# A list of 1250 steps for one core, in another order and with other engines for some of its copies

## The chip, the core and the metric

The kernel runs on one core of a Trainium2 chip. Five engines of that core work side by side, each on its own queue and in the order of that queue: TensorE (PE, matmuls and transposes; PEld in the profile is its weight load), VectorE (DVE), ScalarE (ACT), GpSimd (POOL) and SyncE (SP, here only a queue of DMA issues). The metric is the time of one execution on the device in microseconds; a kernel's time is the median of its runs.

## The reference

Eight batches of eight heads, 576 positions, 64 values per head. Attention is causal, with a bias from the running sum of a per-position gate; its output, as 8 x 576 rows of 512, goes through a layer norm and a two-layer MLP with a residual.

```python
scores = scale * q @ k.T                                  # 8 batches x 8 heads, 576 x 576
cum = cumsum(maximum(s, 0))                               # along the positions
scores = where(causal, -1e9, scores + minimum(-(cum[:, None] - cum[None, :]), 0))
attn = softmax(scores)
x = (attn @ v)  as 8 x 576 x 512                          # heads side by side
xn = (x - mean(x)) / sqrt(var(x) + 1e-6) * g_ln
out = x + maximum(xn @ w_ch1, 0) @ w_ch2                  # 512 -> 2048 -> 512
```

## The kernel before

**The work.** Positions are cut into four tiles of 128 and a tail of 64; the tails of two batches share one tile (`xm`). Batch 0 and 1 put the bias into four extra rows of the key and query matrices. Batches 2 to 7 work with the bias in the values: v is multiplied by a weight per key position (`weigh_v`, L233), two columns behind it hold the weight itself in two parts (`weigh_ones`, L245 and L246), and the sums of these columns divide the result. From batch 2 on, two heads go together as a "burst".

**One burst** `B2.n` (n = 4 x batch + pair): six PSUM banks of scores, transposed, by matmuls (`sa`, `sb`, `sc`, L553); six exponentials on ACT into `er` (`bx`, L560); four causal masks on POOL (`bm`, L497); then for each head P·V into a bank `pot` (`Y`, L626), and its normalization on DVE (`K`: `sums` L643, `rinvs` L644, `xb` L645). The 64-position tails of all heads of a batch have their own steps: copies of the tail keys into a zeroed matrix on POOL (`tk`, L145), matmuls `sd` (L524), an exponential (`se`), a mask (`sm`), P·V (`Z`) and normalization (`z`).

**Loads.** From batch 3 on, f32 rows of q and k come by SP (`lr`, L206, tile `rowtmp`), are cast on POOL (`cr`, L218), and are transposed by DMA (`tr`, L225). v rows come by SP (`lv`, L206, with six buffers) and go through `weigh_v` (`vm`). Earlier batches load by POOL's own DMA queue, and PE transposes them, with copies out of PSUM on ACT or DVE (L141 on ACT, L143 on DVE; words `E`, `G`, `y`, and `O2` for a copy in SBUF ahead of it).

**Norm and MLP.** `ga` are the statistics (L700), `la` one tile's normalization `xn` (L741), `Da` the transposing DMA. An MLP chunk is a queue of 32 units: 16 of "h" (L792, bank `ph`, with a relu into `hT`, L783 on ACT or L781 on DVE) and four times four quarters of "y" (L811, bank `py`, evicted by `yo`, L823, on DVE, and stored by SP). The words `u` and `U` take the next unit of the queue; the letter sets the engine of the relu, and does nothing for a "y" unit. For the first chunk some units are done by tile, as `M` (matmuls) and `r` (relu).

**What sets the order.** Nothing is scheduled: the kernel walks a string of words, `PLAN`, and each word issues its instructions at once to the queues of their engines. A word `name.args:E` names a step of the table `STEPS`; the letter behind the colon is the engine of a copy, a cast or a weighing (A, D, P). So an engine's order is the order of the words. PSUM banks are taken from pools as they come free: until the word `to` there are banks m (2), s (3), t (2), o (1); behind it m (2) for `py`, `pot` and the tails' `pott`, and s (6) for scores, `sd` and `ph`. A word that takes a bank waits on its engine until the bank's last reader is done.

Ahead of the walk, the kernel before issues a prologue of loads and memsets in plain code.

```python
for word in PLAN.split():
    step, _, eng = word.partition(":")
    name, *args = step.split(".")
    args = [int(c) if c.isdigit() else c for c in args]
    STEPS[name](*args, *([E[eng]] if eng else []))
```

## Time and profile before

| | us |
|---|---|
| median of three runs | 345.44 (345.36, 345.44, 347.5) |
| the profiled execution | 344.55 |
| its span on the core | 343.1 |
| around the span | 1.45 |

| engine | busy us | share | instructions |
|---|---|---|---|
| PE | 330.4 | 96% | 3093 |
| DVE | 202.3 | 59% | 568 |
| ACT | 186.5 | 54% | 347 |
| POOL | 167.4 | 49% | 305 |

Times are in microseconds unless marked ns. The profile is of one execution. A row of a group reads: line, engine, operation, what it writes and reads, shapes, count, then the busy time and the mean ns of one, then the engine's idle time just before these instructions and what ended it. A row of a wait reads: who waited, for whom, the sum, how many times, the longest. A row of the chain or the timeline begins with the start and the duration. In a row by stretches, the stretch and its length come first, then each engine's busy time with the number of its instructions, then PE's clock (1.00 is full speed), the share of the DMA engines and GB/s. The granted clock is 0.997 over the span.

### The profile page before, as it was taken

The page shows a single profiled execution, that of the slowest core. Times are in us where ns is not written, and L with a number is a line of the kernel's source. Part 1 is how long each engine was busy: PE and PEld are TensorE (multiplying, and loading weights), DVE is VectorE, ACT ScalarE, POOL GpSimd, SP SyncE. Part 2 cuts the span into 40 slices and gives each one's busy share as a digit, 9 for nine tenths or more (in the row PEclk, how much of TensorE's full clock was granted, in tenths as well). Part 3 has the DMA queues.
Part 4 walks back from the last instruction along what each step waited for, and adds up shares of the span by engine and source line. Part 5 has one row for each costly group of instructions (what it writes and reads, how often), then busy time and mean ns, then how long its engine had stood idle before and what let it go on. Part 6 is the DMA issues. An engine that isn't in the chain of part 4 may idle for free.

```text
span 343.1 us, 8037 instructions
## 1 busy us (share of the span) xinstructions
PE 330.4 (96%) x3093; PEld 183.0 (53%) x3117; DVE 202.3 (59%) x568; ACT 186.5 (54%) x347; POOL 167.4 (49%) x305
## 2 busy tenths in 40 slices
PE   6999999999989999999999999999999999999994
PEld 2899765545544555545555545554455444444443
DVE  6688787957685577357543664566348624533512
ACT  4888899668746676457736774486344204202200
POOL 8897578777379862884774377441301001000000
PEclk9999999999999999999999999999999999999998
DMA  9999999899999999999988976700510141011022
GB/s 142 178 192 182 201 195 208 192 192 253 182 218 213 213 207 201 201 231 214 214 178 201 215 108 151 139 2 2 121 65 2 24 129 46 3 71 51 3 61 66
DMA packets 147962, 48.59 MB, mean 142 GB/s; under 512 B 135280, under 2 KB 143760, under 8 KB 147920
## 3 DMA queue, kind: packets, MB, share of 16 engines
q1 hardware_dynamic: 121856, 38.34, 54.3%
q0 software_dynamic: 24304, 8.92, 22.2%
q10 hardware_dynamic: 1760, 0.79, 1.0%
q8 instruction: 25, 0.41, 0.5%
q14 instruction: 17, 0.14, 0.1%
HBM read 37.11 MB, written 9.44 MB: 136 GB/s over the span
## 4 chain that ended last, share of the span: by engine, by line
PE 72%; POOL 9%; DMA 8%; DVE 4%; SPq 3%; issue 2%; ACT 1%; POOLq 0%; ACTq 0%
PE ph L792 30%; PE py L811 28%; DMA v_bf<-in_v_dram 5%; PE pot L626 4%; SPq L206 3%; PE sa L553 2%; POOL v_bf L233 2%; POOL v_bf L192 1%; DVE xn L741 1%; DMA rowtmp<-in_q_dram 1%; DMA rowtmp<-in_v_dram 1%; ACT er L560 1%; PE sb L553 1%; PE sc L553 1%; PE pott L664 1%
## 5 line engine op out<-in xcount | busy, mean ns | idle before, releaser
L811 PE MATMUL py<-w_bf,hT 128*128 128x512 bf16 (+2 forms) x584 | 128.9, 367 | 2.7 <-DVE yo L823 1.0
L792 PE MATMUL ph<-xT,w_bf 128*128 128x512 bf16 x480 | 109.8, 379 | 0.0
L783 ACT ACTIVATE hT<-ph 128x512 bf16<-128x512 f32 x102 | 60.9, 605 | 78.8 <-PE ph L792 77.1
L811 PEld LDWEIGHTS <-hT 128*128 128x128 bf16 x608 | 55.9, 98 | 60.9 <-issue 1.1
L792 PEld LDWEIGHTS <-w_bf 128*128 128x128 bf16 x544 | 51.4, 98 | 56.4
L497 POOL TENSOR_SCALAR_AFFINE_SELECT er<-er 128x256 bf16<-128x256 bf16 x96 | 38.1, 412 | 52.3 <-ACT er L560 37.7
L823 DVE SCALAR_TENSOR_TENSOR yo<-py,rstd,xb 128x512 f32<-128x512 f32 x32 | 23.9, 749 | 50.7 <-PE py L811 46.2
L560 ACT ACTIVATE er<-sb 128x512 bf16<-128x512 f32 x48 | 28.1, 607 | 20.9 <-PE sb L553 20.9
L781 DVE TENSOR_SCALAR hT<-ph 128x512 bf16<-128x512 f32 x34 | 23.4, 690 | 27.0 <-PE ph L792 25.1
L560 ACT ACTIVATE er<-sa 128x512 bf16<-128x512 f32 x48 | 28.6, 607 | 14.8 <-PE sa L553 14.6
L233 POOL TENSOR_TENSOR v_bf<-rowtmp,wt 128x512 bf16<-128x512 f32 (+1 forms) x30 | 32.9, 1104 | 4.3 <-DMA rowtmp<-in_v_dram 4.1
L560 ACT ACTIVATE er<-sc 128x512 bf16<-128x512 f32 x48 | 28.7, 611 | 4.1 <-PE sc L553 4.1
L741 DVE SCALAR_TENSOR_TENSOR xn<-xb,mv,gb 128x512 bf16<-128x512 f32 x28 | 25.9, 925 | 1.0
L715 POOL TENSOR_TENSOR rstd<-rstd,mhalf 128x4 f32<-128x4 f32 (+1 forms) x8 | 8.8, 1095 | 34.7 <-DVE rstd L714 33.2
L700 DVE BATCH_NORM_STATS2 stats<-xb 128x6 f32<-128x128 f32 (+1 forms) x84 | 24.6, 326 | 0.6
L626 PEld LDWEIGHTS <-er 128*128 128x128 bf16 x480 | 19.7, 97 | 9.5 <-POOL er L497 0.6
L218 POOL CAST kq<-rowtmp 128x512 bf16<-128x512 f32 (+1 forms) x30 | 18.3, 619 | 13.2 <-DMA rowtmp<-in_k_dram 12.3
L643 DVE TENSOR_REDUCE sums<-pot 128x4 f32<-128x8 f32 x48 | 7.8, 162 | 27.0 <-PE pot L626 26.7
L626 PE MATMUL pot<-v_bf,er 128*128 128x66 bf16 x480 | 22.1, 193 | 0.1
L645 DVE TENSOR_TENSOR xb<-pot,rinvs 128x256 f32<-128x256 f32 x48 | 20.4, 424 | 1.7
L553 PEld LDWEIGHTS <-kq 64*128 64x128 bf16 x384 | 11.9, 94 | 9.6 <-issue 3.8
L1017 ACT ACTIVATE er<-st 128x512 bf16<-128x512 f32 x24 | 13.2, 603 | 1.5 <-PE st L1008 1.5
(178 smaller groups left out, 394.8 us busy)
## 6 DMA issues: line engine op xcount, KB each, us to landing
out_dram<-yo SPq DMA_DIRECT2D x32, 256.0 KB
rowtmp<-in_v_dram SPq DMA_DIRECT2D x24, 256.0 KB
rowtmp<-in_k_dram SPq DMA_DIRECT2D x20, 256.0 KB
rowtmp<-in_q_dram SPq DMA_DIRECT2D x20, 256.0 KB
w_bf<-in_moe_w_ch_dram POOLq DMA_DIRECT2D x8, 512.0 KB, 9.2
kp<-in_k_dram POOLq DMA_DIRECT2D x8, 144.0 KB, 9.0
qp<-in_q_dram POOLq DMA_DIRECT2D x8, 144.0 KB, 9.0
v_bf<-in_v_dram POOLq DMA_DIRECT2D x8, 128.0 KB, 7.8
```

The lines of the kernel that those rows point to most:

```text
L233: e.tensor_tensor(out=v_bf[b % 2][0:pn, t, :, 0:D], in0=loaded.pop(("v", b, t))[0:pn], in1=wt[0:pn, t, b, :].unsqueeze(2).to_broadcast([pn ...
L497: nc.gpsimd.affine_select(out=out, in_=out, compare_op=ALU.is_ge, fill=0.0, base=0, pattern=pattern, channel_multiplier=-1,)
L553: nc.tensor.matmul(a, lhsT=lhsT, rhs=rhs, start=True, stop=True)
L560: nc.scalar.activation(out=er[:, 2 * n % 4 + i, o : o + 512], in_=bank["B", n].pop((name, i)), func=ACT.Exp, scale=scale,)
L626: nc.tensor.matmul(pot[:, t, :], lhsT=e[:, o : o + P], rhs=v_bf[b % 2][:, kb, h, :], start=(kb == 0), stop=(kb == t),)
L700: nc.vector.bn_stats(out=st[b][:, t, part, :], in_=x_tiles(b)[t][:, lo:hi])
L741: nc.vector.scalar_tensor_tensor(out=xn, in0=tiles[t], scalar=mvs[b][:, t, 0:1] if b > 0 else mean0[:, t : t + 1], in1=gb, op0=ALU.subtrac ...
L781: nc.vector.tensor_scalar_max(out=dst, in0=ph, scalar1=0.0)
L783: nc.scalar.activation(out=dst, in_=ph, func=ACT.Relu)
L792: nc.tensor.matmul(ph, lhsT=w1_bf[:, kd, fb * P : (fb + 1) * P], rhs=xT[:, :, kd, :], start=(kd == 0), stop=(kd == KD - 1),)
L811: nc.tensor.matmul(py[t], lhsT=hT[:, fb, t * P : (t + 1) * P], rhs=w2_bf[:, fb, c0:c1], start=(fb == 0), stop=(fb == FB - 1),)
L823: nc.vector.scalar_tensor_tensor(out=yo, in0=py[t], scalar=rs, in1=x[:, c0:c1], op0=ALU.mult, op1=ALU.add)
```

## The change

The prologue's loads and memsets become words of the list. They stand as its first 55 words in the order of the code before, and the 37 words behind them are the first 37 of the old list. Behind these 92 the words are the same ones in another order, and some have another engine's letter: 28 copies, casts and weighings, among them fifteen `vm` and four `vo` (batches 2, 3, 4, 6) from POOL to DVE; and of the relu units forty go from ACT to DVE and twenty-four from DVE to ACT. The matmuls are the same.

`piece` takes its bank with whichever of a tile's four column blocks comes first, since they can now stand in any order.

```diff
-    nc.sync.dma_start(out=c_first, in_=s_rows[:, 0 : 2 * P])
-    ld_tile("q", 0, nc.scalar)
-    ld_tile("k", 0, nc.sync)
...
-    ld_cast_tile("k", 1)
-    ld_cast_tile("q", 1)
-    ld_cast_v(0, 0)
...
+    def fill(i):
+        if i == 0:
+            nc.vector.memset(zeros.bitcast(F32), 0.0)
+        elif i == 1:
+            nc.vector.memset(warm, 0.0)
+            nc.scalar.activation(out=warm[:, 1:2], in_=warm[:, 0:1], func=ACT.Exp)
...
+        elif i == 11:
+            nc.gpsimd.memset(rinvs[:, 0, :, NF], 1.0)
+
+    def first_sums(i):
+        if i == 0:
+            nc.sync.dma_start(out=c_first, in_=s_rows[:, 0 : 2 * P])
+        else:
+            nc.sync.dma_start(out=c_in[:, 2 * P : S], in_=s_rows[:, 2 * P : S])
...
-    E = {"A": "act", "D": "dve", "P": "pool"}
+    E = {"A": "act", "D": "dve", "P": "pool", "S": "sync"}
...
     def piece(c, t, j):
-        if j == 0:
+        if ("M", c, t) not in bank:
             bank["M", c, t] = ptile("m", [P, 4, P], "ph")
...
+        "w1": ld_w1,
+        "f": fill,
+        "c": first_sums,
+        "lc": ld_cast_tile,
+        "LV": ld_cast_v,
...
     PLAN = """
-        relu.0 scan.0 relur.1 O cq hi.0 scan.1 ck.0 sub.0 mid.0 lo.0 m hi.1 tc.0 bc.0 sub.1 W.2 T.0.1 relur.2
...
+        c.0 lt.q.0:A lt.k.0:S c.1 f.0 f.1 W.9 f.2 f.3 f.4 f.5 f.6 I lc.k.1 lc.q.1 LV.0.0 lc.k.2 lc.q.2 mT LV.0.1
...
```

**DVE ahead of burst 8** (the first of batch 2). In both pieces `rinvs`, `xb` and `xm0` are the normalization of a head of batch 1 (L602 to L611), `kq1` is a copy of transposed q or k out of PSUM, `stats` the layer norm's statistics. The kernel before:

```order
L143 COPY kq1_110<-trqk_1159 64x2x288
L602 RECIPROCAL rinvs_114<-pot_1215 128x5
L604 TENSOR_TENSOR xb_914<-pot_1215,rinvs_114 128x4x64
L611 TENSOR_SCALAR xm0_117<-pot_1215,rinvs_114 64x64
L718 BN_AGGR mv_222<-stats_221 128x2
L700 BN_STATS stats_1259<-xb_914 128x6
L602 RECIPROCAL rinvs_114<-pot_1261 128x5
L604 TENSOR_TENSOR xb_914<-pot_1261,rinvs_114 128x4x64
L611 TENSOR_SCALAR xm0_117<-pot_1261,rinvs_114 64x64
```

The changed kernel at the same heads:

```order
L781 TENSOR_SCALAR hT_101<-ph_1194 128x512
L602 RECIPROCAL rinvs_114<-pot_1228 128x5
L604 TENSOR_TENSOR xb_946<-pot_1228,rinvs_114 128x4x64
L611 TENSOR_SCALAR xm0_117<-pot_1228,rinvs_114 64x64
L700 BN_STATS stats_1247<-xb_946 128x6
L143 COPY kq1_110<-trqk_1186 64x2x288
L781 TENSOR_SCALAR hT_101<-ph_1250 128x512
L602 RECIPROCAL rinvs_114<-pot_1262 128x5
L604 TENSOR_TENSOR xb_946<-pot_1262,rinvs_114 128x4x64
L611 TENSOR_SCALAR xm0_117<-pot_1262,rinvs_114 64x64
L700 BN_STATS stats_1247<-xb_946 128x6
L781 TENSOR_SCALAR hT_101<-ph_1296 128x512
```

Three relus, which ACT had, now stand between the normalizations.

**POOL ahead of the tails of batch 3.** `c3_122<-kq1_110` are the two copies of the tail keys for which `sd` waits; L233 are weighings of v of batch 3, L218 casts of q and k rows, L497 masks. The kernel before:

```order
L218 CAST kq2_111<-rowtmp_1520 64x512
L497 AFFINE_SELECT er_116<-er_116 128x2x128 x6
L218 CAST rowb_123<-rowtmp_1695 128x512
L497 AFFINE_SELECT er_116<-er_116 128x2x128 x2
L218 CAST rowb_123<-rowtmp_1586 128x512
L233 TENSOR_TENSOR v_bf1_108<-rowtmp_1866,wt_113 128x8x64
L233 TENSOR_TENSOR v_bf1_108<-rowtmp_1921,wt_113 64x8x64
L233 TENSOR_TENSOR v_bf1_108<-rowtmp_1893,wt_113 128x8x64
L145 COPY c3_122<-kq1_110 64x4x64 x2
```

The changed kernel:

```order
L497 AFFINE_SELECT er_116<-er_116 128x2x128 x3
L218 CAST rowb_123<-rowtmp_1631 128x512
L497 AFFINE_SELECT er_116<-er_116 128x2x128
L218 CAST kq2_111<-rowtmp_1520 64x512
L497 AFFINE_SELECT er_116<-er_116 128x2x128 x3
L145 COPY c3_122<-kq1_110 64x4x64 x2
```

No weighing stands ahead of the copies now.

**DVE in batch 5.** `yo` are evictions of the MLP's second layer, `sums`, `rinvs` and `xb` the normalization of a head of batch 4, `v_bf1_108<-rowtmp` a weighing of v of batch 5. The kernel before:

```order
L823 SCALAR_TENSOR_TENSOR yo_2796<-py_2779,rstd_103,xb_1701 128x512
L823 SCALAR_TENSOR_TENSOR yo_2830<-py_2800,rstd_103,xb_1701 128x512
L643 TENSOR_REDUCE sums_2874<-pot_2833 128x4
L644 RECIPROCAL rinvs_114<-sums_2874 128x4
L645 TENSOR_TENSOR xb_2670<-pot_2833,rinvs_114 128x4x64
L643 TENSOR_REDUCE sums_2894<-pot_2883 128x4
L644 RECIPROCAL rinvs_114<-sums_2894 128x4
L645 TENSOR_TENSOR xb_2670<-pot_2883,rinvs_114 128x4x64
```

The changed kernel:

```order
L823 SCALAR_TENSOR_TENSOR yo_2809<-py_2787,rstd_103,xb_1727 128x512
L233 TENSOR_TENSOR v_bf1_108<-rowtmp_2767,wt_113 128x8x64
L643 TENSOR_REDUCE sums_2865<-pot_2854 128x4
L644 RECIPROCAL rinvs_114<-sums_2865 128x4
L645 TENSOR_TENSOR xb_2666<-pot_2854,rinvs_114 128x4x64
L233 TENSOR_TENSOR v_bf1_108<-rowtmp_2743,wt_113 128x8x64
L643 TENSOR_REDUCE sums_2898<-pot_2882 128x4
L644 RECIPROCAL rinvs_114<-sums_2898 128x4
L645 TENSOR_TENSOR xb_2666<-pot_2882,rinvs_114 128x4x64
```

Two weighings, which stood on POOL, are now in DVE's row, each ahead of a normalization.

More of the change, by code (lines that the diff above doesn't have):

```diff
@@ L1318, in fast_path @@
         "lp": ld_cast_pair,
+        "w1": ld_w1,
+        "f": fill,
+        "c": first_sums,
+        "lt": lambda kind, t, eng: ld_tile(kind, t, nc.scalar if eng == "act" else nc.sync),
+        "lc": ld_cast_tile,
+        "LV": ld_cast_v,
+        "I": lambda: make_identity(nc, ident),
+        "mT": make_mask,
+        "g": lambda: nc.gpsimd.dma_start(out=gb, in_=moe_g_ln.partition_broadcast(P)),
+        "cr2": const_rows,
+        "fv": lambda i: nc.gpsimd.memset(v_bf[i][TL:P, NF, :, :], 0.0),
@@ L1319, in fast_path @@
+        "fk": lambda i: nc.gpsimd.memset(kq[i][0:KA, 0, :, S:SP], 0.0),
     }
     PLAN = """
[L1322 to L1325 removed]
```

242 lines of the change are left out of this document (111 added, 131 removed).

## The prediction

> **What bounds the kernel now.** I read the page first: the share of each engine, the slices, the chain that ended last.
>
> ```profile
> span 343.1 us, 8037 instructions
> PE 330.4 (96%) x3093; PEld 183.0 (53%) x3117; DVE 202.3 (59%) x568; ACT 186.5 (54%) x347; POOL 167.4 (49%) x305
> ...
> DMA  9999999899999999999988976700510141011022
> ...
> PE 72%; POOL 9%; DMA 8%; DVE 4%; SPq 3%; issue 2%; ACT 1%; POOLq 0%; ACTq 0%
> ```
>
> TensorE (PE) is busy 96% of the span and is 72% of the chain; no other engine passes 59%. The row of DMA is full up to slice 18 (154 us), so in the first half of the kernel a load can be late. An average over stages hides where an engine is tight, so the second view is the busy time by stretches (the stretch, its length, then PE, PEld, DVE, ACT, POOL).
>
> ```profile
> 0.00:10.00 10.00, 7.36 (x31) 3.44 (x32) 6.27 (x24) 4.61 (x9) 8.86 (x17) 1.00 1.17 150
> 30.00:40.00 10.00, 9.47 (x174) 8.05 (x172) 8.41 (x21) 8.97 (x17) 5.85 (x10) 1.00 1.72 186
> 40.00:50.00 10.00, 10.00 (x145) 7.18 (x144) 8.31 (x20) 9.53 (x21) 6.22 (x14) 1.00 1.26 197
> 50.00:60.00 10.00, 9.72 (x117) 6.04 (x116) 6.95 (x24) 9.18 (x18) 8.53 (x19) 1.00 1.24 207
> 60.00:70.00 10.00, 9.35 (x79) 4.94 (x78) 9.76 (x17) 5.51 (x9) 7.97 (x14) 1.00 0.74 168
> 180.00:250.00 70.00, 69.58 (x649) 36.14 (x650) 39.57 (x117) 42.87 (x81) 31.44 (x59) 1.00 0.58 116
> 330.00:343.10 13.10, 8.42 (x71) 5.45 (x69) 2.70 (x6) 0.00 (x0) 0.00 (x0) 0.93 0.34 81
> ```
>
> This gives a ceiling for any reordering. PE is idle 343.1 − 330.4 = 12.7 us; 10 − 7.36 = 2.64 of that lies in the first 10 us, whose list is the same in both, and 13.10 − 8.42 = 4.68 in the end, where the last output is stored. Left are 5.4 us (a busy PE is not PE at its peak, so this is not exact, but nothing in the rows lets me count more). The set of PE's matmuls doesn't change. The rows also say where others are tight: DVE and ACT from 30 to 70 us, DVE most of all from 60 to 70. From 180 us on, DVE has 30 of 70 us free.
>
> The third view is the chain in order of time, for the two places at which it leaves PE for long.
>
> ```profile
> 58.70 0.42 DVE xb L604
> 59.48 0.81 DVE stats L700 x3
> 60.46 0.80 DVE xn L741
> 61.26 0.41 DVE stats L700 x2
> 61.96 1.65 DVE xn L741
> 63.60 0.80 issue
> 64.71 0.75 DVE yo L823
> 65.64 0.96 DVE xn L741
> 67.11 1.42 DVE xn L741
> 68.53 0.67 DVE kq L143
> 69.20 1.33 DVE yo L823 x2
> 70.57 0.38 PE py L811
> ...
> 90.71 1.77 SPq L206
> 92.53 4.18 DMA rowtmp<-in_v_dram
> 96.77 2.54 POOL v_bf L233 x2
> 99.31 0.81 POOL c L145
> 100.17 0.41 POOL c L145
> 100.63 0.41 PE sd L524 x8
> 101.03 0.86 PE py L811 x4
> ```
>
> At 58.7 to 70.6 us the end hangs on VectorE's (DVE) row: four normalizations, an eviction, a copy, two evictions, with hardly a gap. At 90.7 to 100.6 us a load of v lands, GpSimd (POOL) weighs v, and only behind that, since its row is in order, copies the tail keys for which the `sd` matmuls wait.
>
> **The change, part by part.** The prices come from the groups of instructions (busy time, mean of one) and the waits:
>
> ```profile
> L783 ACT ACTIVATE hT<-ph 128x512 bf16<-128x512 f32 x102 | 60.9, 605 | 78.8 <-PE ph L792 77.1
> L781 DVE TENSOR_SCALAR hT<-ph 128x512 bf16<-128x512 f32 x34 | 23.4, 690 | 27.0 <-PE ph L792 25.1
> L233 POOL TENSOR_TENSOR v_bf<-rowtmp,wt 128x512 bf16<-128x512 f32 (+1 forms) x30 | 32.9, 1104 | 4.3 <-DMA rowtmp<-in_v_dram 4.1
> L741 DVE SCALAR_TENSOR_TENSOR xn<-xb,mv,gb 128x512 bf16<-128x512 f32 x28 | 25.9, 925 | 1.0
> L643 DVE TENSOR_REDUCE sums<-pot 128x4 f32<-128x8 f32 x48 | 7.8, 162 | 27.0 <-PE pot L626 26.7
> L645 DVE TENSOR_TENSOR xb<-pot,rinvs 128x256 f32<-128x256 f32 x48 | 20.4, 424 | 1.7
> L644 DVE RECIPROCAL rinvs<-sums 128x4 f32<-128x4 f32 x48 | 8.6, 179 | 1.6
> L143 DVE COPY xT<-trx 128x512 bf16<-128x512 bf16 x1 | 0.4, 425 | 0.5 <-PE trx L774 0.5
> ...
> POOL v_bf L233 <- DMA rowtmp<-in_v_dram: 4.1, 2, 2.3
> PE sd L524 <- POOL c L145: 1.2, 1, 1.2
> PE pot L590 <- DMA v_bf<-in_v_dram: 0.5, 2, 0.3
> ```
>
> *Loads and memsets as words.* The first 55 words issue what the prologue issued, in its order, and the 37 behind them are unchanged: 0.
>
> *The stall at 100 us.* The POOL piece above shows it: the copies of the tail keys of batch 3 (`c3_122<-kq1_110`) stood behind three weighings of batch 3 and now stand behind masks and casts; of batch 3's five weighings two now run on DVE, the rest come later. The PE wait of 1.2 us goes: −1.2. Next late there would be the masks behind them, at 0.4 us each, within the 0.86 us of a quarter of `py` beside `sd`. If nothing goes, 0.
>
> *More work on DVE before burst 8.* In the row up to the second eviction `yo`, DVE gets three more relus (3 × 0.69 = 2.07), a relu of the first batch's pieces (of the same shape, 0.69), one more `xT` copy (0.43), the eight small operations of two `weigh_ones` (no DVE row for them; by L643 and L644, 0.16 to 0.18 each, 1.4), and a copy of a pair (no DVE row; between 0.43 for the `xT` copy and 0.69, I take 0.6). That is 5.2 us. From 30 to 70 us DVE is busy 8.41 + 8.31 + 6.95 + 9.76 = 33.4 of 40, so 6.6 are free, of which 6.3 before 60. What comes before 55 us (the relus and the `xT` copy, 3.2) I hide in that idle time; the two `weigh_ones` and the pair copy (2.0) fall into the stretch in which the chain runs on DVE without a gap, and land in full. The bounds are 0 and 5.2. ACT gets three relus fewer (3 × 0.605 = 1.8) in a stretch in which it is 92% busy; the chain gives ACT 1%, so I take no gain.
>
> *Slow normalizations.* They take 0.75 us where nothing runs beside them and up to 2.5 where POOL does, as DVE's and POOL's timeline shows:
>
> ```profile
> 60.46 0.80 DVE L741 SCALAR_TENSOR_TENSOR xn<-xb,mv,gb 128x512 bf16<-128x512 f32 x1
> 61.96 2.52 DVE L741 SCALAR_TENSOR_TENSOR xn<-xb,mv,gb 128x512 bf16<-128x512 f32 x1
> ...
> 61.79 1.04 POOL L233 TENSOR_TENSOR v_bf<-rowtmp,wt 128x512 bf16<-128x512 f32 x1
> 62.77 1.16 POOL L218 CAST kq<-rowtmp 128x512 bf16<-128x512 f32 x2
> ```
>
> The four of 58.7 to 70.6 us are 0.80 + 2.52 + 0.96 + 1.42 = 5.7 against 4 × 0.75 = 3.0. POOL keeps casts and two weighings near there but loses the `weigh_ones`; I take a third of the 2.7 us, −0.8 (0 to −2.7).
>
> *Fifteen weighings on DVE.* No DVE row shows one. The nearest is `xn`, also two operands from SBUF and 512 elements: 0.75 to 0.93 us, against 1.1 on POOL. Fifteen take 11 to 14 us, and DVE has the room: 202.3 of 343.1 us are taken. The Trainium skill (SBUF — State Buffer, "Who interferes with whom") states that a DVE operation with two inputs in SBUF and a GpSimd operation that reads SBUF exclude each other, whichever comes first; the row of 2.52 us agrees, and by this rule each moved weighing would go on blocking POOL, or being blocked, which adds to the sum only where the two rows are short of room: at most one mask of 0.41 us at burst 9. What matters more is that DVE's row is in order. The DVE piece above shows the place: the weighing of `rowtmp_2767` now stands ahead of `sums`, `rinvs`, `xb` of the next head and of the next eviction, and in the list only six quarters of `py` (6 × 0.86 = 5.2 us) and a burst of scores lie between its load and it. A load took 1.77 us to issue and 4.18 to land above, 5.95 together, so there is no slack when SP is late, and POOL waited up to 2.3 us for such a load. Counted in the same way, two of the fifteen stand less than 7 us of PE work behind their load, five 9 to 11, eight further. Behind it PE has two quarters of `py` (2 × 0.86) less the 0.77 us of the normalization (0.162 + 0.179 + 0.424), about 1 us of cover. I take +0.5 here (0 to 2.3 − 1.0 = 1.3).
>
> *POOL at burst 21.* Ahead of the mask for which a P·V step of burst 21 waits, POOL now has four casts and a weighing more closely packed (some 3.7 us in a row by 0.6 a cast, `1.16 x2`, and 1.1 a weighing). I take +0.5 (0 to 1.2, the stall that the same kind of queue made at 100 us). The two weighings left on POOL that follow their loads most closely (of batches 3 and 4) have five relu units or more (some 4 us) between them and the P·V steps that need the masks behind them: 0.
>
> *Later first use of v of batch 1.* It stands further behind in PE's order, two units or so; the waits of L590 (0.5 in all) shrink: −0.3 (0 to −0.5).
>
> The relus that change sides behind that (13 more on DVE, 0.69 against 0.605) wait for PE anyway, 77.1 and 25.1 us in their rows: 0. The loads of k and q and the transposes of later batches keep their distance to the bursts that need them within about a unit, 0.86 us; SP's queue is where a delay would start, and its price is that of the loads above: 0 here, the rest in rival B.
>
> Sum: −1.2 + 2.0 − 0.8 + 0.5 + 0.5 − 0.3 = +0.7. The profiled execution took 344.55 us (the span and 1.45 around it), 0.9 below the median of 345.44, so the forecast is 344.55 + 0.7 + 0.9 = **346.1 us**. With all low ends at once the change is −1.2 + 0 − 2.7 + 0 + 0 − 0.5 = −4.4, with all high ends 0 + 5.2 + 0 + 1.3 + 1.2 + 0 = +7.7. The ends won't meet, so I take half the way to each for the forecast's own range: −1.9 to +4.2, 343.6 to 349.6.
>
> **Rivals.** A change below 1%, 3.45 us, can hardly be told from none here; I call faster below 342.0 and slower above 348.9.
>
> *A: the waits go and nothing replaces them.* The stall (−1.2), the normalizations (−2.7), the v waits (−0.5), and the new DVE work finds its idle time: 345.44 − 4.4 = 341.0. For it: 6.6 us free on DVE against 5.2, and the stall plainly goes. Against it: it needs four fifths of all the PE idle time there is in the middle (5.4), while bank evictions stand in the same DVE row. Chance 0.17.
>
> *B: weighings on DVE wait for their loads.* One mechanism: DVE's row stops at a weighing whose `rowtmp` hasn't landed, the evictions `sums`/`xb` and `yo` behind it don't free PE's two banks, PE stops. It costs up to 1.3 us a time beyond the cover; seven of fifteen stand 11 us or less behind their load, and DMA is full up to 154 us. It decides slower when at least three wait in full: 3 × 1.3 + 0.7 = +4.6, 350.0. For it: POOL already waited 4.1 us for v loads in its own row. Against it: two waits only, and eight of the fifteen stand far behind their load. Chance 0.13.
>
> *C: DVE becomes the bound up to burst 9.* All 5.2 us land: −1.2 + 5.2 − 0.3 + 0.5 = +4.2, 349.6. For it: 9.76 of 10 busy at 60 to 70 us. Against it: the added relus stand at 40 to 55 us, with 1.6 to 3 us free in each ten. Chance 0.08.
>
> *D: nothing that shows.* PE's list hides both gains and costs, within half a microsecond of 345.4. It shares its sign with the forecast's neighbours. Chance 0.22; my forecast has the remaining 0.40.
>
> **Numbers.** The forecast's own range, 343.6 to 349.6, with D and C's lower part holds some 0.65; to reach 0.8, the range takes in A's upper and B's lower half: 341.5 to 350.0. Faster by over 1%: A but for its upper part, 0.14, and 0.02 from the forecast's lower end, 0.16. Slower by over 1%: B 0.12, C 0.05 and 0.03 of the forecast's upper end, 0.20. Within 1%: 0.64.
>
> **What would show it.** The `sd` wait on `c L145` at 100 us is absent from the waits. DVE is over 9 in each ten us from 40 to 70 and the DVE stretch of the chain that ends at 70.6 us ends 0.5 to 1.5 us later. A row "DVE v_bf L233 <- DMA rowtmp" with one or two waits, longest below 2.3; with five or more B is right. `xn` means below 0.9. If PE's idle time between 10 and 330 us falls below 2 us, A is right; if it stays at 5 to 6, the forecast is. I am wrong in kind if the difference lies behind 180 us, where I see nothing that could change it.

## The result: slower by two thirds of a per cent, and where it went

The changed kernel takes 347.05 us (median of 22 runs, 346.27 to 349.0); the kernel before took 345.31 in 22 runs of the same occasion (342.69 to 349.68). The ratio is 1.0064, 95% interval 1.0041 to 1.0086: a real loss of about 2 us, within the 1% that was called no change, and inside the forecast's range (346.1, from 341.5 to 350.0). Ratios, and the ranges of runs given further down, leave disturbed runs out (two runs of the experiments took 572 and 610 us), so that a ratio can differ a little from the quotient of the medians.

The profiled execution took 347.48 us, its span is 2.8 us longer than before: PE's last matmul ends 2.3 us later, and the other 0.5 lies behind it. The page's first lines, the answers to those quoted of before:

```profile
span 345.9 us, 8050 instructions
PE 331.7 (96%) x3091; PEld 182.4 (53%) x3117; DVE 225.6 (65%) x618; ACT 176.7 (51%) x328; POOL 149.7 (43%) x274
```

The work moved as the words say: DVE +23 us, POOL −18, ACT −10; PE is the bound as before. For the rest I read one number at each burst: **PE's lag**, the time at which the burst's first `sa` matmul starts, less the time that all of PE's steps ahead of it in the list take at their undisturbed prices (a burst 0.77 us, a P·V 0.30, the tails 0.42 and 0.75, a quarter or a relu unit 0.86, and so on). The matmuls are the same in all kernels, so a step up between two bursts is PE waiting there, or, in four traces of the experiments, PE at half its clock for 3.4 us, which is said where it comes. In us, worked out from the start of those matmuls in each trace:

| burst | 8 | 9 | 12 | 13 | 14 | 16 | 19 | 20 | 31 |
|---|---|---|---|---|---|---|---|---|---|
| before | 9.8 | 10.2 | 10.7 | 12.0 | 12.1 | 12.1 | 12.5 | 12.7 | 13.6 |
| changed | 9.8 | 10.7 | 11.1 | 11.0 | 12.1 | 12.7 | 13.6 | 14.1 | 15.9 |

The step of 1.3 us before burst 13 is gone, and new ones stand elsewhere: 0.5 more than before at burst 9, 1.1 at 14, 0.5 at 15, 0.5 at 19, 0.6 at 20, 0.6 at 25 and 0.2 at 29. With the gain at burst 13, and less some 0.4 of small steps that the kernel before has at the same bursts, they make the 2.3 us at burst 31. The waits of PE of 0.3 us and more in the changed kernel, from 10 us to 330 us:

```profile
PE pot L626 <- DVE v_bf L233: 0.8, 1, 0.8
PE py L811 <- DVE yo L823: 0.8, 1, 0.8
PE pot L626 <- POOL er L497: 0.6, 2, 0.3
PE ph L792 <- DMA xT<-xn: 0.5, 1, 0.5
PE pot L1043 <- ACT er L1002: 0.4, 2, 0.2
PE pot L626 <- DVE xb L645: 0.3, 1, 0.3
```

The `sd` wait isn't among them; P·V (`pot` L626), which waited for nothing worth a row before, now waits for a weighing on DVE, for masks on POOL, and for a bank that a late normalization holds. The largest, at 104.2 us, in the timelines of PE, DVE and POOL of the changed kernel (start, duration, engine):

```profile
104.18 0.23 PE L626 MATMUL pot<-v_bf,er 128*128 128x66 bf16 x2
105.24 0.40 PE L626 MATMUL pot<-v_bf,er 128*128 128x66 bf16 x8 [0.82 <-DVE v_bf L233]
...
99.69 0.75 DVE L233 TENSOR_TENSOR v_bf<-rowtmp,wt 128x512 bf16<-128x512 f32 x1
103.53 1.66 DVE L233 TENSOR_TENSOR v_bf<-rowtmp,wt 128x512 bf16<-128x512 f32 x1
...
102.03 0.60 POOL L218 CAST rowb<-rowtmp 64x512 bf16<-64x512 f32 x1
102.60 2.03 POOL L233 TENSOR_TENSOR v_bf<-rowtmp,wt 128x512 bf16<-128x512 f32 x2
104.60 1.10 POOL L497 TENSOR_SCALAR_AFFINE_SELECT c<-c 64x512 bf16<-64x512 bf16 x1
```

The fifteen weighings on DVE by themselves (min, median, max; first and last start):

```profile
L233 DVE TENSOR_TENSOR v_bf<-rowtmp,wt x15: 670/683/1660, 71.4 to 237.0; 128x512 bf16<-128x512 f32 x13, 64x512 bf16<-64x512 f32 x2
```

The usual one takes 0.68 us; this one took 1.66 while POOL was at two weighings until 104.6, and the first mask behind them took 1.10 (its kind takes 0.65 elsewhere). Below, **the lock** stands for this: a DVE and a POOL operation on SBUF that keep each other waiting. Not all of the 0.82 us is its work. The list has three of the four weighings that this P·V needs directly ahead of it (`vm.3.3:P vm.3.2:P vm.3.1:D bx.13.2 Y.12.0`), and the second one on POOL ends at 104.6; a weighing of 0.68 us on DVE would have ended at 104.2, so that by these rows some 0.6 us are the lock's and the rest the order's.

### The profile page after: what moved, and what is told of

It is laid out like the page before. It is cut to its first block, busy times and chain, and to the rows that moved or that the text cites. A ratio compares the mean times of both kernels' runs of the same rounds, so it can differ in the third digit from the quotient of the medians.

```text
span 345.9 us, 8050 instructions
## 1 busy us (share of the span) xinstructions
PE 331.7 (96%) x3091; PEld 182.4 (53%) x3117; DVE 225.6 (65%) x618; ACT 176.7 (51%) x328; POOL 149.7 (43%) x274
## 5 line engine op out<-in xcount | busy, mean ns | idle before, releaser
L783 ACT ACTIVATE hT<-ph 128x512 bf16<-128x512 f32 x86 | 51.5, 599 | 95.6 <-PE ph L792 93.8
L497 POOL TENSOR_SCALAR_AFFINE_SELECT er<-er 128x256 bf16<-128x256 bf16 x96 | 40.6, 440 | 38.2 <-ACT er L560 31.7
L781 DVE TENSOR_SCALAR hT<-ph 128x512 bf16<-128x512 f32 x50 | 34.0, 688 | 29.2 <-PE ph L792 27.4
L560 ACT ACTIVATE er<-sc 128x512 bf16<-128x512 f32 x48 | 28.2, 614 | 10.1 <-PE sc L553 5.3
L218 POOL CAST kq<-rowtmp 128x512 bf16<-128x512 f32 (+1 forms) x30 | 19.6, 665 | 23.2 <-DMA rowtmp<-in_q_dram 14.4
L741 DVE SCALAR_TENSOR_TENSOR xn<-xb,mv,gb 128x512 bf16<-128x512 f32 x28 | 24.5, 873 | 1.0
L626 PEld LDWEIGHTS <-er 128*128 128x128 bf16 x480 | 19.2, 97 | 10.3 <-issue 1.7
L626 PE MATMUL pot<-v_bf,er 128*128 128x66 bf16 x480 | 22.4, 193 | 2.0 <-DVE v_bf L233 0.8
L233 POOL TENSOR_TENSOR v_bf<-rowtmp,wt 128x512 bf16<-128x512 f32 (+1 forms) x15 | 15.9, 1061 | 5.3 <-ACT hT L783 5.2
L553 PEld LDWEIGHTS <-kq 64*128 64x128 bf16 x384 | 11.9, 94 | 11.0 <-issue 5.8
L218 POOL CAST rowb<-rowtmp 128x512 bf16<-128x512 f32 (+1 forms) x20 | 12.3, 630 | 4.5 <-DMA rowtmp<-in_k_dram 4.4
```

Of the source, the lines that this page charges most:

```text
L218: nc.gpsimd.tensor_copy(out=rows[b % 2][0:pn, t, u], in_=loaded.pop(("kq"[u], b, t))[0:pn])
L497: nc.gpsimd.affine_select(out=out, in_=out, compare_op=ALU.is_ge, fill=0.0, base=0, pattern=pattern, channel_multiplier=-1,)
L560: nc.scalar.activation(out=er[:, 2 * n % 4 + i, o : o + 512], in_=bank["B", n].pop((name, i)), func=ACT.Exp, scale=scale,)
L626: nc.tensor.matmul(pot[:, t, :], lhsT=e[:, o : o + P], rhs=v_bf[b % 2][:, kb, h, :], start=(kb == 0), stop=(kb == t),)
L741: nc.vector.scalar_tensor_tensor(out=xn, in0=tiles[t], scalar=mvs[b][:, t, 0:1] if b > 0 else mean0[:, t : t + 1], in1=gb, op0=ALU.subtrac ...
L781: nc.vector.tensor_scalar_max(out=dst, in0=ph, scalar1=0.0)
```

## The experiments

All of them change words of the list or one instruction; the line numbers are those of the kernel that was edited. Lags at the same bursts, one trace each. With the words of the kernel before up to burst 8, kernels reach it with lags of 8.0 to 9.9, so a difference of 2 us there says little, and the steps say more:

| | 8 | 9 | 12 | 13 | 14 | 16 | 19 | 20 | 31 |
|---|---|---|---|---|---|---|---|---|---|
| before | 9.8 | 10.2 | 10.7 | 12.0 | 12.1 | 12.1 | 12.5 | 12.7 | 13.6 |
| before, a second trace | 8.9 | 8.9 | 9.5 | 11.1 | 11.2 | 11.3 | 12.1 | 14.8 | 15.7 |
| tails first | 9.7 | 9.7 | 10.3 | 10.2 | 12.5 | 12.5 | 12.9 | 13.4 | 14.3 |
| tails first, xn later | 8.6 | 8.6 | 9.1 | 9.1 | 9.2 | 9.9 | 10.5 | 14.8 | 15.7 |
| the same, second trace | 8.7 | 8.8 | 10.1 | 10.0 | 10.6 | 10.9 | 11.3 | 15.6 | 16.5 |
| three parts | 8.0 | 8.0 | 8.6 | 8.5 | 8.6 | 9.2 | 9.7 | 9.6 | 10.5 |
| the same, second trace | 9.9 | 9.9 | 10.5 | 10.4 | 10.5 | 11.8 | 13.3 | 14.0 | 14.9 |
| before with weighings on DVE | 9.7 | 9.7 | 11.6 | 11.9 | 12.0 | 12.0 | 12.4 | 12.3 | 13.2 |
| before, one operand in `xn` | 9.8 | 9.9 | 10.4 | 11.6 | 11.7 | 11.7 | 12.1 | 12.6 | 13.5 |
| changed | 9.8 | 10.7 | 11.1 | 11.0 | 12.1 | 12.7 | 13.6 | 14.1 | 15.9 |
| changed, six places mended | 9.5 | 10.2 | 10.5 | 10.4 | 11.0 | 11.8 | 13.8 | 13.7 | 15.1 |
| changed, weighings back | 10.1 | 11.5 | 15.8 | 15.7 | 17.8 | 17.9 | 19.7 | 20.6 | 23.0 |
| changed, early relus back | 11.8 | 12.5 | 12.8 | 12.8 | 13.9 | 14.5 | 15.2 | 15.4 | 16.8 |
| changed, all engines as before | 12.5 | 13.2 | 17.4 | 17.3 | 21.1 | 21.2 | 22.6 | 23.4 | 28.4 |

### Order and engines apart

First, the changed kernel's order with weighings and `weigh_ones` back on POOL:

```diff
- vm.2.2:D vm.2.1:D vm.3.0:D vm.3.1:D vm.4.3:D vm.4.4:D vm.5.1:D vm.5.3:D vm.5.0:D vm.5.2:D
- vm.6.3:D vm.6.1:D vm.6.4:D vm.7.0:D vm.7.3:D vo.2:D vo.3:D vo.4:D vo.6:D
+ (the same words, in the same places, with :P)
```

> The changed kernel with its fifteen weighings and four weigh_ones back on POOL, and nothing else undone: its order and its relus stay. Theory (weighings and weigh_ones in DVE's row cost PE about 1.9 us, at 70.4, 110.8 and 142.0 us; but the order lists those of batch 3 so late that POOL needs them in a row): those three gaps go, the gap at 104.2 us grows from 1.0 to about 2 us, and the kernel takes 346.1 (345.5 to 346.7). Rival 1 (the order is at fault and the engine isn't): 347.0 or more, the gaps stay with POOL as the one waited for. Rival 2 (all of the loss comes from DVE's weighings): 345.0 or less.

It takes 351.0 us (median of five runs; ratio to before 1.0144, 1.0087 to 1.0201). The trace is of the slowest of the five, 354.1 us, so its steps are larger than the median's. Its longest waits of P·V:

```profile
PE pot L626 <- POOL v_bf L233: 3.8, 2, 2.0
PE pot L626 <- POOL er L497: 1.8, 2, 0.9
```

The steps are 4.0 us between bursts 9 and 10 (11.5 to 15.5), 2.1 at burst 14, 1.5 at 19. Of the 4.0, 2.0 are P·V of burst 8 waiting for a weighing, and most of the rest is the clock: from 79.2 us on, right behind this wait, the trace has PE's granted clock at 0.5 for 3.4 us. So neither the theory (346) nor rival 2 held, and rival 1 (347.0 or more) held but was too mild: in this order a weighing on DVE isn't the fault but what holds the order up.

Then the same order with every letter of the kernel before, relus and copies too:

> The changed kernel's order with every engine letter of the kernel before: weighings, weigh_ones, relus and copies. Theory (the new order lists weighings of v late and rests on DVE's doing half of them): as with only the weighings back, the P.V steps of bursts 8, 12 and 20 wait 1 to 2 us each for POOL; 350.5 (349 to 352). Rival (it was the mix of engines that cost, the order is neutral): 345 to 346.

357.8 us (median of four runs, 355.2 to 359.8), ratio 1.0373 (1.0322 to 1.0425): 7 us worse still, above the theory's range and far from the rival's. Of PE's five waits of over 1 us in its trace, which is of the slowest run, one is for `yo` and four are P·V steps waiting for POOL (2.2, 1.8, 1.4 and 1.6 us, of bursts 8, 12, 20 and 23), and twice the clock falls to 0.5 for 3.4 us at such a wait, at 79.3 and at 113.5 us. And the other half by itself, the old order with the nineteen letters:

```diff
- (fifteen vm and four vo of the list before, with :P)
+ (the same words, in the same places, with :D)
```

> The kernel before, in its own order, with the same fifteen weighings and four weigh_ones on DVE. In this order weighings stand close behind their loads. Theory (a weighing on DVE that waits for its load stops the evictions behind it; this was rival B of the prediction): two or more waits of DVE L233 on DMA rowtmp of 1 to 2.3 us, about 1 us of them reaching PE each, the stall of sd gone in part; 346.5 (345.5 to 348). Rival (DVE has the room, and POOL is relieved): the stall of 1.35 us goes and nothing comes: 344.0.

344.6 us, ratio 0.9975 (0.9940 to 1.0010). The time is nearer the rival's than the theory's. The stall of `sd` is gone, and the mechanism of rival B shows once, in DVE's timeline and PE's:

```profile
93.71 0.69 DVE L233 TENSOR_TENSOR v_bf<-rowtmp,wt 128x512 bf16<-128x512 f32 x1 [1.45 <-DMA rowtmp<-in_v_dram]
94.31 0.16 DVE L643 TENSOR_REDUCE sums<-pot 128x4 f32<-128x8 f32 x1
94.72 0.42 DVE L645 TENSOR_TENSOR xb<-pot,rinvs 128x256 f32<-128x256 f32 x1
...
95.20 0.32 PE L664 MATMUL pott<-v_bf,er 128*64 128x66 bf16 x8 [1.11 <-DVE xb L645]
```

DVE stops 1.45 us at a load, the normalization behind it frees its bank late, PE stands 1.1 us. It is one such wait of fifteen weighings, not three or more; it costs what the stall of `sd` gave. What follows from the three: the new order with the old letters costs 13 us, the nineteen letters in the old order nothing measurable, and the new order with all of its letters 2 us. Neither half can be priced without the other. The new order with the nineteen letters and the old relus and copies wasn't run.

### The early work on DVE

```diff
- u U u U U U U U u r.0.2:D        (units 0, 3, 5, 8, 9, 10, 12, 13, 18 of the list)
+ U u U u u u u u U r.0.2:A
```

> The changed kernel with the relus of the first chunk, up to burst 8, on the engines that they had before (nine units and one block relu). Theory (what DVE got there is hidden in its idle time, as the trace of the changed kernel shows at burst 8): PE reaches burst 8 within 0.2 us of the changed kernel, and the time is 347.0 within half a microsecond. Rival C of the prediction (DVE bounds the stretch up to burst 9): PE is 0.5 to 2 us earlier at burst 9, and the time is 346 or less.

348.1 us (two runs; ratio 1.0117, 1.0083 to 1.0152), and PE is 2.0 us later at burst 8 in its one trace, not equal and not earlier. Both expectations missed. PE stands 1.3 us up to 41.9 us, where a relu that this puts on DVE comes ahead of two copies out of PSUM: DVE waits 1.54 us for the relu's bank, and the copies come 1.6 to 1.9 us later than in the changed kernel. A second wait, 0.9 us at 67.3 us, is for `yo`. PE's waits in this run and DVE's timeline:

```profile
PE pot L1043 <- DVE kq L143: 1.3, 1, 1.3
...
37.08 0.69 DVE L781 TENSOR_SCALAR hT<-ph 128x512 bf16<-128x512 f32 x1 [1.54 <-PE ph L792]
38.93 0.81 DVE L143 COPY kq<-trqk 64x576 bf16<-64x576 bf16 x1
41.09 0.78 DVE L143 COPY kq<-trqk 64x576 bf16<-64x576 bf16 x1
```

In the changed kernel the same copies stand at 37.07 and 39.45, each before PE needs it. That the 5 us which DVE got there are hidden rests on the traces of the changed kernel (9.8 at burst 8, as before) and not on this run, which puts two relus on DVE as well as taking others off; what it shows is that one relu of 0.69 us in the wrong place of the same stretch isn't hidden.

### The stall of `sd`, taken away by itself

```diff
- cr.4.0.1 vm.3.1:P Y.11.1
+ cr.4.0.1 tk.3 vm.3.1:P Y.11.1
...
- bx.12.0 vm.3.2:P tk.3
+ bx.12.0 vm.3.2:P
```

> The kernel before with one word moved: the copies of the tail keys of batch 3 go on POOL ahead of the first weighing of batch 3 instead of behind three of them. Theory (the stall of 1.35 us of PE at 99 us is caused by POOL's row alone, and PE has no slack behind it): the wait of sd on c L145 goes, PE is 1.3 to 1.4 us earlier from burst 13 to the end, and the kernel takes 345.3 - 1.3 = 344.0 us. Rival (the stall only hides the next one, since the masks and casts behind the copies come later): PE is back at its old place by burst 16 and the time stays at 345.3.

344.7 us, ratio 0.9991 (0.9951 to 1.0032): nothing. The step before burst 13 is gone as expected (10.3 to 10.2), and 2.3 us come back at burst 14. That is what the rival said, by another wait than its masks and casts. DVE's and POOL's timelines of this run:

```profile
98.52 4.67 DVE L741 SCALAR_TENSOR_TENSOR xn<-xb,mv,gb 128x512 bf16<-128x512 f32 x1
103.42 0.75 DVE L823 SCALAR_TENSOR_TENSOR yo<-py,rstd,xb 128x512 f32<-128x512 f32 x1
...
96.69 2.54 POOL L233 TENSOR_TENSOR v_bf<-rowtmp,wt 64x512 bf16<-64x512 f32 x2 [2.14 <-DMA rowtmp<-in_v_dram]
99.19 0.40 POOL L497 TENSOR_SCALAR_AFFINE_SELECT er<-er 128x256 bf16<-128x256 bf16 x1
99.55 1.16 POOL L218 CAST rowb<-rowtmp 128x512 bf16<-128x512 f32 x2
100.67 0.40 POOL L497 TENSOR_SCALAR_AFFINE_SELECT er<-er 128x256 bf16<-128x256 bf16 x1
101.04 1.03 POOL L233 TENSOR_TENSOR v_bf<-rowtmp,wt 128x512 bf16<-128x512 f32 x1
102.03 0.60 POOL L218 CAST rowb<-rowtmp 128x512 bf16<-128x512 f32 x1
102.60 1.21 POOL L497 TENSOR_SCALAR_AFFINE_SELECT er<-er 128x256 bf16<-128x256 bf16 x2
```

One normalization `xn` lasted 4.67 us instead of 0.75: from its start until 102.6 us POOL has seven operations without a gap between them, and the `xn` ends at 103.2, about when the eighth, a mask, does. The eviction `yo` stands behind it, and PE waited 1.5 us for `yo`. This names a cause that isn't in any wait: DVE counts as busy. That POOL makes an `xn` long, all traces say: of the 468 normalizations with two operands in 13 traces, the 210 with no POOL operation beside them took 0.75 us each, and all 124 over 0.8 us had one beside them.

### Is it the lock, and does it matter where it falls?

Two `xn` go behind the evictions that they stood ahead of (on top of the edit before):

```diff
- la.2.0 la.2.1 cr.4.0.0
+ la.2.0 cr.4.0.0
...
- bm.12.0 u u sd.3
+ bm.12.0 u la.2.1 u sd.3
...
- ga.2.0.2 la.2.2 u
+ ga.2.0.2 u
...
- ga.2.2.3 u u la.2.3
+ ga.2.2.3 u la.2.2 u la.2.3
```

> The kernel before with the tail-key copies first, and two normalizations xn of batch 2 behind the evictions yo that they stood ahead of. In the run without the second part one xn lasted 4.67 us, as long as POOL worked without a gap beside it, and yo, PE's bank, came only behind it. Theory (POOL's row of masks, casts and weighings keeps DVE out of operations with two operands in SBUF, and PE loses time only where an eviction stands behind such an operation): xn is still 2 us or more, the PE gap of 1.69 us at 102.3 us and the one of 0.5 at 105.7 go, PE is 2 us earlier at burst 31, and the kernel takes 343.0 (342.3 to 343.7). Rival (the gap belongs to the weighings of v, and comes back at burst 12's P.V): 344.5 or more.

344.4 us, ratio 0.9986 (0.9950 to 1.0022). The step of 2.3 us at burst 14 is 0.1 (9.1 to 9.2), but the longest `xn` is 1.6 us where 2 or more was expected, so this trace doesn't show whether a long one would have been harmless. A later trace with the same two words does (three parts, the second trace):

```profile
99.60 3.67 DVE L741 SCALAR_TENSOR_TENSOR xn<-xb,mv,gb 128x512 bf16<-128x512 f32 x1
```

There an `xn` took 3.67 us, and the lag at burst 14 rises by 0.1 (10.4 to 10.5): in that place a long `xn` cost PE nothing. But the time doesn't follow: in the trace of this run the lag jumps by 4.3 us at burst 20. P·V of burst 18 waits 2.6 us for a mask, and the matmuls behind it run slow:

```profile
147.01 1.03 PE L792 MATMUL ph<-xT,w_bf 128*128 128x512 bf16 x4
150.60 0.47 PE L626 MATMUL pot<-v_bf,er 128*128 128x66 bf16 x10 [2.57 <-POOL er L497]
150.91 2.44 PE L792 MATMUL ph<-xT,w_bf 128*128 128x512 bf16 x6
```

Four matmuls take 1.03 us ahead of the wait, six take 2.44 behind it. The trace has the granted clock at 0.5 from 151.2 us on, for 3.4 us; that is the other 1.7 us of the jump.

The other question, whether it is the second operand in SBUF that makes `xn` slow, went to the kernel before with the mean's subtraction only; the multiplication by the layer norm's weight is left out:

```diff
-        nc.vector.scalar_tensor_tensor(out=xn, in0=tiles[t], scalar=mean, in1=gb,
-            op0=ALU.subtract, op1=ALU.mult)
+        nc.vector.tensor_scalar(out=xn, in0=tiles[t], scalar1=mean, scalar2=None,
+            op0=ALU.subtract)
```

> The kernel before with xn as subtraction of the mean alone: the multiplication by the layer norm's weight is left out, so that xn has one operand in SBUF instead of two, and nothing else changes. Theory (xn is slow beside POOL because of its second operand in SBUF): no xn lasts over 0.9 us (before: up to 2.5), the sum over the base falls from 6 us to below 1, PE's lag up to burst 9 is 0.5 to 1 us less, and the time is 344.3 (343.5 to 345.0), the stall at 99 us staying. Rival (it is not the second operand; anything of DVE is slow beside POOL): the long ones stay, and the time is 345.2.

343.8 us, ratio 0.9983 (0.9957 to 1.0009). The `xn` of this run, of before, and of tails first (min, median, max, first and last start):

```profile
L741 DVE TENSOR_SCALAR xn<-xb,mv x28: 486/487/1215, 61.2 to 270.6; 128x512 bf16<-128x512 f32 x28
```

```profile
L741 DVE SCALAR_TENSOR_TENSOR xn<-xb,mv,gb x28: 751/752/2519, 60.5 to 271.4; 128x512 bf16<-128x512 f32 x28
```

```profile
L741 DVE SCALAR_TENSOR_TENSOR xn<-xb,mv,gb x28: 750/752/4667, 60.9 to 272.1; 128x512 bf16<-128x512 f32 x28
```

The time lies in the range of the theory, but isn't told from before, and the theory missed in the trace: an `xn` is faster, 0.49 us, and still up to 1.2 us beside POOL, and the sum over the base is 4.2 us (before 6.3), not below 1. The run doesn't tell the second operand from the rest, since the one-operand form isn't free of POOL either. The Trainium skill (SBUF — State Buffer, "Who interferes with whom") says that a DVE instruction with two inputs in SBUF contends with a GpSimd instruction that reads SBUF, that `tensor_scalar` can contend too, in a mode that uses the shared ports, and that the one that comes second waits for the whole of the other's instruction. The three rows agree with that, and the 4.67 us goes beyond it: there DVE waited through a whole row of instructions, not for one.

### Six repairs of the changed kernel

```diff
- vo.3:D                                    + vo.3:P
- bx.13.5 vm.3.3:P vm.3.2:P vm.3.1:D        + vm.3.1:D ahead of la.2.1, the two :P ahead of cr.4.1.0
- bx.14.3 vo.4:D                            + vo.4:D behind K.13.0
- bm.18.2 vm.5.3:D                          + vm.5.3:D behind K.17.1
- bm.18.0 Da.3.0                            + Da.3.0 ahead of lr.6.0
- cr.7.0.1 ahead of Y.23.1                  + cr.7.0.1 behind K.23.0
```

> The changed kernel with six repairs, each at one of the new PE gaps of its trace: weigh_ones of batch 3 back on POOL (gap of 0.94 us at 70.4 us, PE waits for yo); one weighing of batch 3 up ahead of a normalization on DVE, and two on POOL ahead of two casts (0.99 at 104.2, P.V waits for a weighing on DVE that lasted 1.66 beside two weighings on POOL); weigh_ones of batch 4 behind two normalizations of heads (0.51 at 110.8); one weighing of batch 5 behind two normalizations (0.49 at 142.0, P.V waits for a mask); the transposing DMA of xn of batch 3 ahead of two loads (0.66 at 150.0); a cast of batch 7, which waited 9.1 us for its load, behind the masks (0.41 at 197.0). Theory (each gap has its own cause, and PE, which has no slack, keeps what is won): four of the six gaps go at least, PE is 2.5 to 3.5 us earlier at burst 31, and the kernel takes 347.0 - 3 = 344.0 us (343.5 to 344.5). Rival (gaps are handed on to the next wait): PE is less than 1.2 us earlier at burst 31 and the time is above 345.8.

346.1 us, ratio to before 1.0013 (0.9985 to 1.0042): about 1 us won of the 3 expected (0.8 in the lag at burst 31; the ratio of the changed kernel was 1.0064). Four of the six gaps are gone or halved (bursts 14, 15, 20, 25). The one at 70.4 us stays although `weigh_ones` of batch 3 is back on POOL, so that alone wasn't its cause. Two new ones stand ahead of 121.6 (a step of 0.7 us) and of 142.6 (1.7). The second is the lock again, at another `xn`:

```profile
136.94 3.54 DVE L741 SCALAR_TENSOR_TENSOR xn<-xb,mv,gb 128x512 bf16<-128x512 f32 x1
140.66 1.19 DVE L741 SCALAR_TENSOR_TENSOR xn<-xb,mv,gb 128x512 bf16<-128x512 f32 x1
141.77 0.74 DVE L823 SCALAR_TENSOR_TENSOR yo<-py,rstd,xb 128x512 f32<-128x512 f32 x1
```

Its rival was right: at four places the repairs work, and much of the gain is lost again at the next wait.

### Who holds PE at burst 18

Theory after these runs: loads pace POOL around 130 to 145 us, weighings of batch 5 follow, and the masks of burst 18 come behind them at 150 us or later, whatever PE won before. The third part takes the weighings of batches 4 to 7 off POOL:

```diff
- vm.4.3:P vm.4.4:P vm.5.0:P vm.5.1:P vm.5.2:P vm.5.3:P vm.6.1:P vm.6.3:P vm.6.4:P vm.7.0:P vm.7.3:P
+ vm.4.3:D vm.4.4:D vm.5.0:D vm.5.1:D vm.5.2:D vm.5.3:D vm.6.1:D vm.6.3:D vm.6.4:D vm.7.0:D vm.7.3:D
```

> The kernel before with the tail-key copies first, the two xn of batch 2 behind the evictions, and eleven of the fifteen weighings (those of batches 4 to 7) on DVE as the changed kernel has them. Without the third part PE won 3 us up to burst 19 and lost them at 147.7 us, where P.V of burst 18 waited 2.6 us for a mask; ahead of that mask POOL had casts, whose loads came at the pace of the DMA queue, then weigh_ones and four weighings of batch 5. Theory (POOL's queue from those loads on sets when the mask comes, at 150 us whatever PE won before; without the weighings the mask comes some 3 us sooner): no gap over 0.6 us at bursts 18 to 20, PE's lag at burst 31 is 11 to 12.5 us (before 13.6), and the kernel takes 343.3 (342.5 to 344.0), faster than both. Rival (the loads alone set it): the lag is back at 12.5 or more at burst 20 and the time is 344.5 or more.

The profiled execution took 341.85 us, the lag at burst 20 is 9.6 and at burst 31 10.5, with no gap over 0.6 us behind 70 us, all better than expected. But the median of its runs is 343.92 (ratio 0.9982, 0.9950 to 1.0013), inside the expected range and not told from before. How far one trace speaks for a kernel, a second run of three programs shows:

> The kernel before once more, for a second trace of one program. Single runs of it lie between 342.6 and 349.5 us, and kernels with the same list up to burst 8 reached it with PE lags of 8.0 to 9.8 us. Theory (what differs between runs of one program comes mostly from the loads of the first 70 us): the lag at burst 8 differs from 9.8 by up to 2 us, and the steps from burst 12 on repeat within 0.3 us, the stall of sd (1.3 us) among them. Rival (the waits of the middle part are chance too): the stall of sd is absent or another gap of over 0.5 us stands between bursts 12 and 20.

> The kernel of the three parts once more: its profiled run was the fastest of its runs. Theory (its middle part has no gap, and only the start varies): lag from burst 12 to burst 31 grows by 1.9 us within 0.3 (before: 2.9). Rival (the first trace was a lucky one): a gap of over 0.6 us is back between bursts 12 and 31.

> The kernel with the first two parts once more: its profiled run had the gap of 2.7 us at burst 18. Theory (the mask of burst 18 comes at a time that loads and POOL's weighings set, so that what PE won before is lost there): P.V of burst 18 waits again for the mask, until 150 to 151 us; the earlier PE is at burst 18, the longer. Rival (chance): no wait over 0.5 us there.

They took 346.6, 346.0 and 347.5 us, one run each. The kernel before, unchanged, has in its second trace the same gap that the edit seemed to have brought. POOL's timeline of this second trace, up to the mask, and PE's:

```profile
145.81 0.61 POOL L218 CAST rowb<-rowtmp 128x512 bf16<-128x512 f32 x1 [2.18 <-DMA rowtmp<-in_q_dram]
146.94 1.04 POOL L233 TENSOR_TENSOR v_bf<-rowtmp,wt 128x512 bf16<-128x512 f32 x1
148.31 1.04 POOL L233 TENSOR_TENSOR v_bf<-rowtmp,wt 128x512 bf16<-128x512 f32 x1
149.67 1.04 POOL L233 TENSOR_TENSOR v_bf<-rowtmp,wt 128x512 bf16<-128x512 f32 x1
150.67 1.58 POOL L497 TENSOR_SCALAR_AFFINE_SELECT er<-er 128x256 bf16<-128x256 bf16 x3
...
152.30 0.47 PE L626 MATMUL pot<-v_bf,er 128*128 128x66 bf16 x10 [2.67 <-POOL er L497]
```

And the same masks in the first trace of the three parts, where the weighings are on DVE:

```profile
142.25 0.61 POOL L218 CAST kq<-rowtmp 128x512 bf16<-128x512 f32 x1
142.82 2.73 POOL L497 TENSOR_SCALAR_AFFINE_SELECT er<-er 128x256 bf16<-128x256 bf16 x5
```

In this pair the late load differs as well as the weighings. Cleaner is the first trace of before beside that of before with weighings on DVE: the cast with the late load starts at 144.2 and 144.3, and the masks are done at 150.2 with the weighings on POOL and at 148.3 without. So the gap at burst 18 isn't what the edit cost: with the weighings on POOL, P·V of that burst starts at 150 to 152 us in the traces at hand (150.6, 150.8, 151.5 and 152.3 where it waited; 150.2 in the first trace of before, where PE came just then). What PE had won before is lost in that wait. The theory of the last expectation held (P·V waits again, until 151.5), though the first trace of before shows that the wait can be absent. In the first expectation the rival held: not only the start varies between runs, since the step at burst 20 is 0.2 us in one trace of before and 2.7 in the other, where the load of the cast came 1.7 us later. For the three parts the rival holds too: in the second trace its P·V of burst 18 doesn't wait, yet it loses 1.3 us ahead of burst 18 (0.9 of it a P·V waiting for a mask) and 0.8 ahead of burst 20 (the transposing DMA of `xn`), and so gives 346.0. That it is faster than both kernels isn't shown; its runs lie at 341.85 to 345.04, before's in the same occasion at 342.83 to 347.17. What the spread comes from is open: the first 70 us (lags of 8.0 to 9.9 at burst 8 in kernels with the same words up to there, `weigh_ones` apart), the loads at 130 to 146 us, and the clock, which fell to 0.5 at burst 18 in both traces of the kernel with the first two parts and in none of the other two programs'.

## Why the prediction was right, and where its steps were not

The sum said +0.7 us and 346.1; measured were 347.05 and a ratio worth 2.2 us, on the same side and inside the range. The size is right in part by luck: terms that were too large and waits that were in no term lie against each other. By its steps:

- **Loads and memsets as words**: 0 forecast; PE is busy 7.36 us of the first ten before and 7.31 changed. (Of the 37 old words behind them 36 are in place, and `qu.2` stands where `x.0.1.0` stood.)
- **The stall of `sd`**: −1.2 forecast, −1.4 at burst 13 in the lag. Right, and right about POOL's row as the cause. Not foreseen: taken away alone it is worth nothing, since a long `xn` takes it back (tails first).
- **More work on DVE before burst 8**: +2.0 forecast; measured 0.07 us at burst 8, which is less than two traces of one kernel differ there, and 0.5 at burst 9, where PE waits 0.8 us for `yo` behind two `xn`. The step at burst 9 is 0.7 us or more in all five traces of the new order and 0.4 or less in all others, so it is the order's. The term was too large by 1.5: most of what I made land in full fitted in. Whether ACT's lighter load gained anything no run shows: with the old relus PE is 2.0 us later, but its new waits there are for DVE.
- **Slow normalizations**: −0.8 forecast; the four ahead of burst 9 took 0.75 + 0.90 + 0.75 + 1.27 = 3.7 us instead of 5.7, and the mean of all 28 fell from 925 to 873 ns (the row below). How much of this reaches PE can't be told apart from the term above; the two together were +1.2 and measured +0.5.

```profile
L741 DVE SCALAR_TENSOR_TENSOR xn<-xb,mv,gb 128x512 bf16<-128x512 f32 x28 | 24.5, 873 | 1.0
```

- **Weighings on DVE**: the price was nearly right (forecast 0.75 to 0.93 us; the median is 0.68, the fifteen together 12.0 us of a forecast 11 to 14), and none waits for its load in this trace. The place (`vm.5.3`) was right and gave 0.5 us as forecast, but by another mechanism: DVE didn't wait for the load, it held up a mask on POOL (0.85 us instead of 0.41) for which P·V waited, as the timelines show:

```profile
140.99 1.18 DVE L233 TENSOR_TENSOR v_bf<-rowtmp,wt 128x512 bf16<-128x512 f32 x1
...
141.58 0.85 POOL L497 TENSOR_SCALAR_AFFINE_SELECT er<-er 128x256 bf16<-128x256 bf16 x1
...
142.49 0.32 PE L626 MATMUL pot<-v_bf,er 128*128 128x66 bf16 x5 [0.32 <-POOL er L497]
```

  The step that failed is "which adds to the sum only where the two rows are short of room: at most one mask of 0.41 us at burst 9". At burst 14 the step was 1.1 us, the lock and the late place of three weighings together, and in tails first the step behind the long `xn` was 2.3.
- **POOL at burst 21**: +0.5 forecast, 0 measured there; two bursts later, at 195 us, POOL stood 9.1 us at a cast whose load was late, and a P·V waited 0.2 us for a mask behind it, in a step of 0.6 at burst 25. A queue that is long isn't one that is late. Late loads were taken to end at 154 us, where the row of DMA was read as full; it shows 8 or 9 up to slice 23 (197 us) and 6 or more up to slice 26 (223 us).
- **v of batch 1**: −0.3 forecast; no wait of L590 for a load over 0.3 us stands in any of the five traces of the new order; in the nine of the old order such waits sum to 0 to 1.1 us. Right, as small as it is.
- **Not in the sum**: `weigh_ones` of batch 4 ahead of a normalization (0.5), and the transposing DMA of batch 3 behind two loads in SP's queue (0.6; "0 here, the rest in rival B" was the sentence). With the 1.1 at burst 14 and the steps at bursts 25 and 29 (0.6 and 0.2), 3.0 us stood in no term. The terms above came to 1.1 less than forecast, and the small steps of the kernel before are to be taken off: 0.7 + 3.0 − 1.1 − 0.4 = 2.2, near the 2.3 in the lag.

Of the signs that were named, the `sd` wait is gone and the mean of `xn` is below 0.9 us. DVE is busy 8.15, 9.35 and 9.57 us in the three tens from 40 to 70, so not over 9 in each. A wait of a DVE weighing for its load, of which one or two were expected, is absent. PE's idle time between 10 and 330 us is 6.4 us (before 5.4), a little above the 5 to 6. And 0.8 of the 2.3 us arose behind 180 us, at bursts 25 and 29, where the prediction saw nothing that could change; by its own words it was wrong in kind for that third.

Rival A did not come: waits went, others replaced them. B's mechanism exists (weigh alone), once and in the old order; the changed kernel has no such wait. C is refuted by the lags at bursts 8 and 9. The ceiling of 5.4 us kept the forecast from promising a large gain; it says nothing of a loss, and the same order with the old letters lost 13 us. Of the terms, three were off by half a microsecond or more.

## What to carry to other kernels

A stall that ends at PE is worth its length only if nothing paced from elsewhere stands behind it, so look whether the next waits come at a fixed time (loads, a queue behind loads) before counting a gain. When an order and a choice of engines were made together, neither can be priced alone: here the order with the old letters cost 13 us, nineteen of the letters in the old order nothing, order and letters together 2. And compare several traces of the same program before blaming an edit for a gap: a gap of 2.7 us appeared in a second trace of the unchanged kernel. Where PE is slow behind a wait, read the granted clock of that stretch before looking for a second wait.

## What the hardware did that was not expected

- A DVE operation on SBUF can be kept out through a row of POOL operations that follow one another without a gap: 4.67, 3.67 and 3.54 us for an `xn` of 0.75, beside seven or eight POOL operations (tails first, the second trace of the three parts, six places). It shows as a long busy DVE row, not as a wait.
- It works the other way too: masks on POOL took 0.85 and 1.10 us instead of 0.41 and 0.65 while DVE was at a weighing. In all 14 traces, the 1185 masks of `er` without an `xn` or a weighing on DVE beside them took at most 0.43 us, and all 72 over 0.5 us had one beside them.
- At five waits of PE of 1.8 to 2.6 us, in four traces, the granted clock fell to 0.5 for 3.4 us, and matmuls of 512 columns came 0.43 us apart instead of 0.22. At a wait of 2.7 us in the second trace of before it stayed at 1.00, so the length of the wait alone doesn't decide it.
- The same words up to burst 8 reached it with lags of 8.0 to 9.9 us, and the kernel before reached burst 31 with 13.6 and 15.7 in its two traces.
